# Issuing 28 stores of a two-layer spectral and MLP kernel from GpSimd in place of SyncE

## The chip, the cores and the metric

The kernel runs on one core of a Trainium2 chip. The metric is the device time of one execution in microseconds (us). The kernel before took 1453.88 us as the median of three runs, which lay between 1451.45 and 1456.33 us.

## What is computed

The reference applies two different blocks in turn, and the pair of them twice (two "layers"). `S` is 2048 tokens, `D` is 512 channels, everything is fp32.

```python
# block A: Fourier mixing, real part of a DFT over tokens of a DFT over channels
a = einsum("bsd,ed->bse", x, dft_hid_re);  b = einsum("bsd,ed->bse", x, dft_hid_im)
y = einsum("ts,bse->bte", dft_seq_re, a) - einsum("ts,bse->bte", dft_seq_im, b)
# block B: spatial shift and MLP
h  = gelu(layernorm(x) @ w1);  hs = concat(four quarters of h, shifted by +1, -1, +2, -2) @ w2
x1 = x + hs
x  = x1 + gelu(layernorm(x1) @ w3) @ w4          # w3: 512 x 1376, w4: 1376 x 512
# x = x + A(layernorm(x)); x = x + B(layernorm(x)); and both once more
```

## The kernel before

**Precision.** Every fp32 operand of a product is split into a rounded high part, written by ScalarE (ACT) as `fp32r`, and a low part, the operand less its high part, written by VectorE (DVE). One product is then three matmuls (high by high, high by low, low by high; `mm3`, L343 to L345). TensorE (PE) therefore has almost all of the work, and DVE and ACT feed it with splits, with sums and with gelu.

**Seven products in place of eight.** The large products are done on 2 x 2 blocks with seven block products in place of eight. Each needs sums of the blocks of its operands, here called forms. For the Fourier block of layer 1 the right operand is the DFT matrix of the channels (`hs`, its real and imaginary part). Its seven forms never change, so the kernel computes them once, beside other work, splits each into high and low, and keeps the results in device memory, in the tensors `hsd`. Layer 1 loads them from there (`rawr<-hsd`, from 801 us on).

**Where that is done.** The second half of a layer, the MLP with `w3` and `w4`, goes through the tokens in two pairs of chunks (`by_pairs`). In the second pair of layer 0 PE walks through the 11 blocks of `w3`, two columns at a time: for each it does seven products with `w3b` (`prod`, in the order b1, b6, b5, b2, b7, then two blocks of the product with `w4`, then b4, b3). DVE adds the seven results up out of PSUM (`rest`, L567), ACT applies gelu (L763) and splits. Between these products the code calls `one()`, which takes the next item of a list of background work, `bg`. The seven forms are on that list: `hs_forms` makes them in four quarters, and each quarter (`hs_quarter`) has one load step and five parts. In each quarter:

- `load_m` (L1208) loads the imaginary part's block into `m`, `load_r` (L1211) the real part's into `r`, 256 KB each. There is one buffer of each per quarter, and the four quarters' buffers lie at the same addresses, so a load waits until the quarter ahead has read its last values out of them.
- `sums` (L1214 to L1217, by the helper at L567) makes the sums, three of them in the buffers `hp0`, `hp1` and `hp2` (the list `fp`; the name in the trace is `hp`, its first digit the buffer and its second the quarter). These too lie at the same addresses in all quarters.
- four parts follow, which `outs` makes. Each has a step `highs_` (ACT, L1224) and a step `lows_` (DVE, L1229), and `lows_` also issues the store of the finished form to `hsd` (L1230). The parts use `hp1, hp2, hp0`, then `hp1, hp2`, then `hp0`, then `hp1`: seven forms through three buffers. A buffer is written again only when the store from it has landed, so ACT waits for stores within a quarter, and the first sum of the next quarter (into `hp1`) waits for the seventh store of the quarter ahead.

Each store moves 128 rows of 2 KB, 256 KB; there are 28 of them. The list `bg` carries the highs and lows beside steps that prepare layer 1 (`xp_stats`, `xp_norm`, `ax_sums` and so on). Of these `xp_stats` ends on GpSimd (POOL) with two small operations on a 128 x 2 tile (L362, L363), whose results ACT needs for L391.

**Queues.** Every engine works through its instructions in order. All transfers before the change are issued by SyncE (SP), in the order of the code: a transfer whose data isn't ready holds up all that stand behind it in SP. In this part SP also issues the loads of `w4` (`w4r<-w4d`, L943, 512 KB each), of `w3` (`w3b<-w3d`, L958, 1792 KB each) and the two loads of `hs`. In the code, the next quarter's `load_m` is called right behind the sixth store, and `load_r` right behind the seventh.

Of the kernel before, what the change touches and what calls it, by code (L numbers as in the profile page):

```python
# [8 lines left out]
F32 = mybir.dt.float32  # L9
# [36 lines left out]
def spectral_mlp_kernel(ctx: ExitStack, tc: tile.TileContext, x, ws, hs, w1, w2, w34, out):  # L46
    nc = tc.nc
# [110 lines left out]
    def piece(src, a=0, b=2):  # L158
        pieces.append((src, a, b))
        return len(pieces) - 1  # L160
# [25 lines left out]
    for layer in range(LAYERS):  # L186
        for c in range(NC):
# [15 lines left out]
            for k in range(NP):  # L203
# [4 lines left out]
                p = piece(ws[c, k][:, 2:4])  # L208
# [357 lines left out]
    def add(o, a, b, op=ALU.add):  # L566
        nc.vector.tensor_tensor(o, a, b, op=op)  # L567
# [290 lines left out]
    def by_pairs(layer, zs, xin, dst):  # L858
# [344 lines left out]
        def hs_quarter(m, r, fp, places):  # L1203
            b11, b12, b21, b22 = (t[:, :, v] for t in (m, r) for v in (left, right))
            raw = [tf[:, :, 1] for _, tf in fp]

            def load_m():
                nc.sync.dma_start(m, places[0][1])  # L1208

            def load_r():  # L1210
                nc.sync.dma_start(r, places[0][2])  # L1211

            def sums():
                add(raw[1], b12, b11, ALU.subtract)  # L1214
                add(raw[2], b22, b12, ALU.subtract)
                add(raw[0], b22, raw[1], ALU.subtract)
                add(b12, raw[0], b21, ALU.subtract)  # L1217

            def outs(*which):
                which = [(i, n, raw[i] if src is None else src) for i, n, src in which]  # L1220

                def highs_():
                    for i, _, src in which:
                        act(fp[i][0][:, :, 0], src)  # L1224

                def lows_():
                    for i, n, src in which:
                        t = fp[i][0]
                        nc.vector.tensor_tensor(t[:, :, 1], src, t[:, :, 0].bitcast(F32), op=ALU.subtract)  # L1229
                        nc.sync.dma_start(places[n][0].rearrange("p i (l w) -> p i l w", l=2), t.bitcast(F32))  # L1230

                return highs_, lows_

            nothing = lambda: None
            parts = [
                (nothing, sums),
                outs((1, 3, None), (2, 4, None), (0, 2, None)),
                outs((1, 0, b11), (2, 1, b12)),
                outs((0, 6, b21)),
                outs((1, 5, b22)),  # L1240
            ]
            return [(load_m, load_r), *parts]
# [15 lines left out]
        for pair in range(n_pairs):  # L1258
# [62 lines left out]
            for p in range(NF // 2):  # L1321
                prep = {} if kept else w_prep(p)
                u, v, x, y = sets[p % 2]
                w = w3b[(5 * pair + p) % 2]
# [835 lines left out]
```

## Time and profile before

| | us |
|---|---|
| median of three runs | 1453.88 |
| profiled execution | 1454.98 |
| span from its first to its last instruction | 1452.9 |
| PE busy | 1420.9 |
| DVE busy | 1204.9 |
| ACT busy | 731.8 |
| POOL busy | 76.6 |

The profiled execution gives all durations. Times inside it count from the start of the span. A row such as `647.65 0.39 SPq L1230 DMA_DIRECT2D hsd<-hp x1` gives the start, the duration in us, the engine (`SPq` is SyncE's queue of instructions), the line of the kernel, the operation, the tile written and the tile read, and how many instructions were merged. In brackets behind a row stands how long the engine was idle before it, and what ended the idle time. The issue of a transfer is short; when its data has landed is told apart, as the time from issue to landing. In the chain of waits a row with `DMA` is a transfer on its way, from issue to landing.

### The profile page before, as it was taken

Reading aid. Unit: us, or ns where it says so; the run is one execution under the profiler, and the core shown is the slowest. Engines: PE = TensorE matmul, PEld = TensorE weight load, DVE = VectorE, ACT = ScalarE, POOL = GpSimd, SP = SyncE. Lnnn points to the kernel's source line nnn. Section 1 sums busy time; section 2 is a strip of 40 time slices with the busy share of each in tenths; the row PEclk is TensorE's granted clock in tenths of the full one; section 3 lists DMA queues with packets and bytes.
Section 4 is the critical chain, followed back from the end, with each engine's and each line's share of the span. In section 5 each row is a group of like instructions: output and inputs, shape, how many; then the busy total and the mean of one; then the engine's idle time right before and its main releaser. Section 6 shows DMA issues by size and latency. Waiting matters only on the chain.

```text
span 1452.9 us, 18506 instructions
## 1 busy us (share of the span) xinstructions
PE 1420.9 (98%) x6681; PEld 1188.4 (82%) x6681; DVE 1204.9 (83%) x1725; ACT 731.8 (50%) x1020; POOL 76.6 (5%) x105
## 2 busy tenths in 40 slices
PE   9999999999999999998999989989989999999999
PEld 7888888888888888876888878878878888899887
DVE  7986998989978897667799878879879797897676
ACT  5663554445566654344555443444445666444342
POOL 2100000000002000000000000000000011000000
PEclk9999999999999999999999999999999999999999
DMA  7867657568645758877655577576687537586864
GB/s 247 274 204 234 200 173 261 173 200 296 226 133 161 268 214 282 329 251 263 232 173 190 203 256 225 187 269 222 207 294 240 173 102 275 165 250 217 320 205 163
DMA packets 145628, 325.24 MB, mean 224 GB/s; under 512 B 10624, under 2 KB 61568, under 8 KB 142848
## 3 DMA queue, kind: packets, MB, share of 16 engines
q1 hardware_dynamic: 145536, 324.05, 66.9%
q8 instruction: 53, 0.87, 0.2%
q14 instruction: 39, 0.32, 0.1%
HBM read 262.41 MB, written 61.60 MB: 223 GB/s over the span
## 4 chain that ended last, share of the span: by engine, by line
PE 83%; DVE 9%; DMA 4%; ACT 2%; issue 2%; SPq 0%; DVEq 0%; ACTq 0%
PE psd L343 8%; PE psd L345 8%; PE psd L344 8%; PE psa L343 7%; PE psa L344 7%; PE psa L345 7%; PE psb L344 6%; PE psb L343 6%; PE psb L345 6%; PE psc L344 6%; PE psc L345 6%; PE psc L343 6%; DVE ring L300 1%; DVE rest L567 1%; DMA raw<-in_ws 1%
## 5 line engine op out<-in xcount | busy, mean ns | idle before, releaser
L300 DVE TENSOR_TENSOR ring<-raw,ring 128x1024 fp32r<-128x1024 f32 x102 | 124.2, 1220 | 19.0 <-ACT ring L279 18.7
L279 ACT CAST ring<-raw 128x1024 fp32r<-128x1024 f32 x103 | 107.8, 1051 | 56.3 <-PE psd L345 25.6
L383 POOL TENSOR_TENSOR rs<-ve,mhalf 128x4 f32<-128x4 f32 x16 | 25.0, 1562 | 746.1 <-DVE nm L382 746.1
L343 PE MATMUL psd<-ring,ay 128*128 128x512 f32 x126 | 50.1, 398 | 7.8 <-DVE tmp L567 7.8
L300 DVE TENSOR_TENSOR ring<-ring1f,ring 128x512 fp32r<-128x512 f32 (+1 forms) x56 | 53.3, 952 | 2.9 <-ACT ring L282 2.9
L286 ACT CAST ring<-ring0f 128x1024 fp32r<-128x1024 f32 x28 | 29.5, 1053 | 50.5 <-DVE ring0f L285 50.2
L286 ACT CAST ring<-ring2f 128x1024 fp32r<-128x1024 f32 x28 | 29.6, 1056 | 48.8 <-DVE ring2f L285 48.8
L343 PE MATMUL psd<-rawr,hf 128*128 128x256 f32 x168 | 47.7, 284 | 5.8 <-issue 4.8
L343 PE MATMUL psc<-ring,ay 128*128 128x512 f32 x128 | 50.2, 392 | 2.0 <-ACT rr11f L608 1.7
L300 DVE TENSOR_TENSOR ring<-ring3f,ring 128x1024 fp32r<-128x1024 f32 (+1 forms) x50 | 49.3, 986 | 3.0 <-ACT ring L282 2.6
L362 POOL TENSOR_TENSOR rs<-ve,mhalf 128x2 f32<-128x2 f32 (+2 forms) x33 | 29.2, 886 | 426.6 <-DVE nb L361 407.6
L391 ACT ACTIVATE tmp<-xs,nb,rs 128x512 f32<-128x512 f32 x56 | 43.3, 810 | 15.8 <-POOL nb L363 12.6
L344 PE MATMUL psb<-ring,ay 128*128 128x512 f32 x128 | 50.3, 393 | 0.8 <-DVE ring L300 0.8
L343 PE MATMUL psb<-ring,ay 128*128 128x512 f32 x128 | 50.5, 394 | 0.0
L345 PE MATMUL psb<-ring,ay 128*128 128x512 f32 x128 | 50.1, 391 | 0.0
L345 PE MATMUL psd<-ring,ay 128*128 128x512 f32 x126 | 49.9, 396 | 0.0
L344 PE MATMUL psc<-ring,ay 128*128 128x512 f32 x128 | 49.8, 389 | 0.0
L345 PE MATMUL psc<-ring,ay 128*128 128x512 f32 x128 | 49.8, 389 | 0.0
L344 PE MATMUL psd<-ring,ay 128*128 128x512 f32 x126 | 49.8, 395 | 0.0
L344 PE MATMUL psa<-ring,ay 128*128 128x512 f32 x126 | 49.0, 389 | 0.0
L343 PE MATMUL psa<-ring,ay 128*128 128x512 f32 x126 | 49.0, 389 | 0.0
L345 PE MATMUL psa<-ring,ay 128*128 128x512 f32 x126 | 49.0, 389 | 0.0
(896 smaller groups left out, 4757.8 us busy)
## 6 DMA issues: line engine op xcount, KB each, us to landing
raw<-in_ws SPq DMA_DIRECT2D x183, 512.0 KB, 5.2
w4r<-w4d SPq DMA_DIRECT2D x44, 512.0 KB, 5.3
rawr<-hsd SPq DMA_DIRECT2D x42, 512.0 KB, 4.8
w3b<-w3d SPq DMA_DIRECT2D x10, 1792.0 KB, 9.3
raw<-in_hs SPq DMA_DIRECT2D x32, 512.0 KB, 4.0
w3d<-w3b SPq DMA_DIRECT2D x5, 1792.0 KB, 7.0
hsd<-hp SPq DMA_DIRECT2D x28, 256.0 KB, 2.4
x1d<-tmp SPq DMA_DIRECT2D x12, 512.0 KB, 7.4
```

Source lines behind the costliest of these rows:

```text
L279: nc.scalar.copy(dest[:, a:b, 0], r[0][:, a:b])
L286: nc.scalar.copy(dest[:, :, 0], lo)
L300: nc.vector.tensor_tensor(lo, src, hi.bitcast(F32), op=ALU.subtract)
L343: nc.tensor.matmul(o, lh, rh, start=first, stop=False, skip_group_check=more)
L344: nc.tensor.matmul(o, lh, rl, start=False, stop=False, skip_group_check=more)
L345: nc.tensor.matmul(o, ll, rh, start=False, stop=last, skip_group_check=more)
L362: nc.gpsimd.tensor_tensor(rs[:, :n], ve[:, :n], mhalf[:, 0, :n], op=ALU.pow)
L383: nc.gpsimd.tensor_tensor(rs, ve, mhalf[:, :, :2], op=ALU.pow)
L391: nc.scalar.activation(o, s, AF.Identity, bias=mr[2], scale=mr[1])
L567: nc.vector.tensor_tensor(o, a, b, op=op)
```

## The change

The stores at L1230 are issued by GpSimd. The operation, the data and the place in the code stay; nothing else in the kernel is edited.

```diff
                     for i, n, src in which:
                         t = fp[i][0]
                         nc.vector.tensor_tensor(t[:, :, 1], src, t[:, :, 0].bitcast(F32), op=ALU.subtract)
-                        nc.sync.dma_start(places[n][0].rearrange("p i (l w) -> p i l w", l=2), t.bitcast(F32))
+                        nc.gpsimd.dma_start(places[n][0].rearrange("p i (l w) -> p i l w", l=2), t.bitcast(F32))
```

PE, DVE and ACT keep their instructions in the same order. SP loses 28 transfers and POOL gains them. This is what stands on SP in the second quarter; `hsd_95` and the like are the seven forms, `hp_4396` is `hp1`, `hp_4398` is `hp2`, `hp_4394` is `hp0`, `hs_4400` is the next quarter's `m` and `hs_4401` its `r`.

```order
-L1230 DMA hsd_95<-hp_4396 128x512
-L1230 DMA hsd_97<-hp_4398 128x512
-L1230 DMA hsd_93<-hp_4394 128x512
-L1230 DMA hsd_89<-hp_4396 128x512
-L1230 DMA hsd_91<-hp_4398 128x512
 L943 DMA w4r_251<-w4d_114 128x1024
-L1230 DMA hsd_101<-hp_4394 128x512
 L1208 DMA hs_4400<-in_hs 128x512
 L943 DMA w4r_253<-w4d_115 128x1024
-L1230 DMA hsd_99<-hp_4396 128x512
 L1211 DMA hs_4401<-in_hs 128x512
 L958 DMA w3b_236<-w3d_86 128x3584
```

Five loads of the quarter stay on SP in their order, and no store stands between them; what `load_m` and `load_r` waited for by their place behind a store they now wait for by semaphores of DVE. On POOL the same seven stores now stand between the statistics of two steps:

```order
 L362 TENSOR_TENSOR rs<-ve,mhalf 128x2
 L363 TENSOR_TENSOR nb<-nb,rs 128x2
+L1230 DMA hsd_95<-hp_4396 128x512
+L1230 DMA hsd_97<-hp_4398 128x512
+L1230 DMA hsd_93<-hp_4394 128x512
+L1230 DMA hsd_89<-hp_4396 128x512
+L1230 DMA hsd_91<-hp_4398 128x512
+L1230 DMA hsd_101<-hp_4394 128x512
+L1230 DMA hsd_99<-hp_4396 128x512
 L362 TENSOR_TENSOR rs<-ve,mhalf 128x2
 L363 TENSOR_TENSOR nb<-nb,rs 128x2
```

The stores are queued behind the two operations of their own quarter's statistics and ahead of those of the next quarter. The other three quarters look the same.

## The prediction

> **What bounds the kernel now.** The page first: PE has almost no idle time over the whole span.
>
> ```profile
> span 1452.9 us, 18506 instructions
> PE 1420.9 (98%) x6681; PEld 1188.4 (82%) x6681; DVE 1204.9 (83%) x1725; ACT 731.8 (50%) x1020; POOL 76.6 (5%) x105
> ```
>
> So a change can gain only where PE waits. The stretches around the stores come next: busy time of each engine from the first store's quarter to the last one's, and behind it.
>
> ```profile
> 612.00:690.00 78.00, 70.35 (x299) 56.47 (x298) 56.05 (x122) 37.44 (x73) 4.01 (x8) 0.98 0.69 246
> 690.00:800.00 110.00, 109.97 (x485) 90.46 (x484) 98.57 (x141) 59.05 (x82) 6.25 (x8) 1.00 0.59 197
> ```
>
> PE (first figure after the length) idles 78.00 - 70.35 = 7.65 us in the part with the stores and not at all in the 110 us behind it. What is won or lost by 690 therefore stays. The timeline of PE shows the five waits:
>
> ```profile
> 642.23 0.50 PE L343 MATMUL psa<-b,w3b 128*128 128x512 f32 x1 [0.66 <-DVE rest L567]
> 647.25 0.50 PE L343 MATMUL psa<-bt,w3b 128*128 128x512 f32 x1 [0.63 <-DVE rest L567]
> 661.48 0.50 PE L343 MATMUL psa<-b,w3b 128*128 128x512 f32 x1 [3.05 <-DVE rest L567]
> 666.50 0.50 PE L343 MATMUL psd<-bt,w3b 128*128 128x512 f32 x1 [0.65 <-DVE rest L567]
> 680.33 0.79 PE L343 MATMUL psd<-b,w3b 128*128 128x512 f32 x1 [2.67 <-DVE rest L567]
> ```
> ```profile
> 680.00:690.00 10.00, 9.67 (x36) 7.85 (x37) 7.88 (x16) 7.18 (x14) 0.00 (x0) 0.83 0.63 209
> ```
>
> All wait for DVE's additions out of PSUM. The last wait has a second price: in the ten us from 680 on the granted clock (third figure from the end) is 0.83, so of the 9.67 us that PE is busy 0.17 x 9.67 = 1.6 us are lost.
>
> DVE is late because it waits itself. Its waits in this part, and the longest of them in its own timeline:
>
> ```profile
> DVE hp12f L567 <- DMA hsd<-hp: 3.7, 1, 3.7
> DVE hp13f L567 <- DMA hsd<-hp: 3.2, 1, 3.2
> DVE hp11f L567 <- DMA hsd<-hp: 2.4, 1, 2.4
> ```
> ```profile
> 645.84 0.75 DVE L1229 TENSOR_TENSOR hp<-hs,hp 128x256 fp32r<-128x256 f32 x2
> ...
> 653.82 0.43 DVE L567 TENSOR_TENSOR hp12f<-hs 128x256 f32<-128x256 f32 x1 [3.72 <-DMA hsd<-hp]
> ```
>
> At the turn of each quarter DVE must rewrite `hp1`, and the seventh store has not left it. At the second turn the last low is ready at 645.84 + 0.75 = 646.59 and the next quarter begins at 653.82. SP and the chain of waits show where these 7.23 us go:
>
> ```profile
> 646.29 0.32 SPq L1230 DMA_DIRECT2D hsd<-hp  x1
> 646.66 0.42 SPq L1208 DMA_DIRECT2D hs<-in_hs  x1
> 647.18 0.38 SPq L943 DMA_DIRECT2D w4r<-w4d  x1
> 647.65 0.39 SPq L1230 DMA_DIRECT2D hsd<-hp  x1
> 648.09 0.47 SPq L1211 DMA_DIRECT2D hs<-in_hs  x1
> 648.66 0.44 SPq L958 DMA_DIRECT2D w3b<-w3d  x1
> ```
> ```profile
> 629.65 4.66 DMA hsd<-hp
> ...
> 648.09 6.22 DMA hs<-in_hs
> ```
>
> The store waits 1.06 us for its turn on SP behind a store and two loads, and is then about 6 us on its way, since those transfers are ahead of it. `load_r`, issued behind it, lands at 654.31, just as late. At the first turn the store took 4.66 us.
>
> **The change, part by part.** No operation is added or removed; 28 issues move from SP to POOL. On SP they cost 0.36 us each and land in 2.0 us at the least:
>
> ```profile
> L1230 SPq DMA_DIRECT2D hsd<-hp x28: 319/357/411, 619.7 to 685.3; - x28
> DMA to landing us min/median/max: 2.0/2.4/6.0
> ```
>
> SP's 28 x 0.36 = 10 us are worth nothing by themselves; no engine waits in this part for the `w4` and `w3` loads that come earlier. What counts are `load_m` and `load_r`. `load_m` needs only forms 4 and 5, so it and the `w4` load go some 2 us earlier, and `load_r` goes as soon as the last low is read. It is no longer late.
>
> The **price of a store on POOL** stands in no row, since POOL issues nothing now. Nearest rows: the operations of the same queue.
>
> ```profile
> L362 POOL TENSOR_TENSOR rs<-ve,mhalf 128x2 f32<-128x2 f32 (+2 forms) x33 | 29.2, 886 | 426.6 <-DVE nb L361 407.6
> L383 POOL TENSOR_TENSOR rs<-ve,mhalf 128x4 f32<-128x4 f32 x16 | 25.0, 1562 | 746.1 <-DVE nm L382 746.1
> ```
>
> The bounds are 0.36 us (as on SP, landing in 2.0) and 1.56 us (landing in 2.0 + 1.56 - 0.36 = 3.2). I take 0.89 us, the row of the operation that POOL does between these very stores, and so 2.0 + 0.89 - 0.36 = 2.53 us to landing.
>
> *Within a quarter this costs.* The first store stands behind the statistics, which it did not on SP, and ACT waits for the buffers:
>
> ```profile
> 620.34 0.20 POOL L363 TENSOR_TENSOR nb<-nb,rs 128x2 f32<-128x2 f32 x1
> 639.62 0.20 POOL L363 TENSOR_TENSOR nb<-nb,rs 128x2 f32<-128x2 f32 x1
> ```
> ```profile
> 621.90 0.41 ACT L1224 CAST hp<-hs 128x256 fp32r<-128x256 f32 x1 [3.19 <-DMA hsd<-hp]
> 622.48 0.41 ACT L1224 CAST hp<-hs 128x256 fp32r<-128x256 f32 x1 [0.17 <-DMA hsd<-hp]
> ...
> 642.74 0.70 ACT L1224 CAST hp<-hs 128x256 fp32r<-128x256 f32 x2
> ...
> 645.67 0.41 ACT L1224 CAST hp<-hs 128x256 fp32r<-128x256 f32 x1 [0.50 <-DMA hsd<-hp]
> ```
>
> First quarter: stores from 620.54, 621.43; the second lands at 623.96, and the cast of 622.48 starts at 624.05, 1.55 us late. All behind it on ACT and DVE slips as much. PE doesn't wait in this quarter, so I count nothing for it here; without that slack it would be 1.55 us. Later quarters have work in front of the casts: with stores from 639.82 on the second lands at 643.24 (needed at 643.05, 0.3 late), and the fourth, ready at 643.59, at 646.1, so that the cast of 645.67 is 0.5 late. The last low is then ready at 647.1 and not 646.59. POOL's own next statistics come some 9 us after the seventh store's issue and lose nothing; stores of over 2 us each would reach them, and ACT's normalisation (L391) behind them.
>
> *At the turn it gains.* The seventh store starts on POOL at 647.6, behind the sixth. Alone it lands at 650.1. But `w3b`, 1792 KB, now leaves SP right behind `load_r`, also at 647.6, and nothing holds it back. How long it fills the queues:
>
> ```profile
> w3b<-w3d SPq DMA_DIRECT2D x10, 1792.0 KB, 9.3
> ```
> ```profile
> 652.00:658.00 6.00, 6.00 (x28) 4.99 (x27) 3.95 (x12) 1.02 (x3) 0.01 (x1) 1.00 0.91 379
> ```
>
> At 379 GB/s it takes 1.835 MB / 379 = 4.8 us. If its data start 1 us after the issue and all go first, the store lands at 648.6 + 4.8 + 1.2 = 654.6. The turn then ends between 650.2 (3.6 early) and 654.7 (0.9 late). No row says how two queues share; I take the middle, 652.5, **1.3 us early**. The first turn by the same steps: last low at 630.4, the seventh store from 630.4 lands between 632.9 and 638.0, middle 635.5, where it landed at 629.65 + 4.66 = 634.31: 1.2 late.
>
> The Trainium skill has a rule for this, "DMA: Bandwidth & Descriptors", section "Issuing engines are not separate DMA queues": transfers from all engines run on the same 16 DMA engines and interleave, and issuing from several saves only the sequencers' time. By it nothing but the 1.06 us of SP's turn is to be had at each turn, 3 us at most in all, and the store doesn't overtake for free. The 379 GB/s row, with the DMA engines 0.91 busy, leaves little room for a transfer beside `w3b`, so far in agreement.
>
> *Sum.* The third turn comes 1.2 - 1.3 - 1.3 = 1.4 us earlier than before, and PE's last wait ends with it, as its first matmul follows the turn by a fixed chain. PE's third and fourth waits shrink, but the second and fourth grow by the 0.5 of the casts; the last one is left with about 1 us. Whether the 1.6 us of the lower clock go with it is open: behind the longer wait at 661.48 the matmul took 0.50, not 0.79. I count 0.6. Together -2.0 us: 1454.98 - 2.0 = 1453.0 for the profiled execution, which lay 1.1 above the median, so **1452**.
>
> **Rivals.**
>
> *The store keeps ahead of `w3b`* (the low end). Then the turns come 1.4, 5 and 8.6 us earlier, DVE leads, and nearly all of the 7.65 + 1.6 us go; less 1.8 for what the casts still cost, 7.5: 1446. For it: the sixth store and `load_r` go first too. Against: `w3b` is issued at the same moment.
>
> *`w3b` goes first.* Turns 3.7, 4.6 and 5.5 late: 1459.
>
> *POOL is the bound*: its issues come one behind another, three at the start of each quarter, and two casts wait for them. At 1.56 us the first quarter's cast is 2.9 late and the later lows 2.1; the seventh store is issued 2 us later. With the middle share the turns come 3.6, 4.8 and 6.0 late: 1460, **slower**. Between -1.4 at 0.89 us and +6.0 at 1.56 it decides at about 1.0 us per store. For it: ACT already waits 3.19 us for a store. Against: SP's 0.36.
> The Trainium skill, "SBUF — State Buffer", section "SBUF: two separate sides", holds that GpSimd can't write its descriptors while DVE runs an operation that takes both ports. By it the price rises above 1.0 us. The quoted DVE rows here have two inputs, and no run here shows such a lock, so it has a small part of this rival.
>
> *Nothing changes*: stores land as before and `load_r` too. The span stays within 1 us: 1454.
>
> **How the numbers follow.** The forecast has 0.40 (1447 to 1455), the store ahead 0.20, `w3b` first 0.14, POOL the bound 0.22, no change 0.04. A measurement of this kernel tells about 0.3%, 4.4 us, from no change. Faster by more: 0.20 and 0.10 of the forecast, 0.30. Slower by more: 0.20 of POOL's and 0.09 of `w3b` first, 0.29. The rest, 0.41, is within. The range runs from the store ahead, 1445, to POOL's price at its upper bound, 1461.
>
> **What would show it.** Right: POOL's stores about 0.9 us apart, landing in 2.5 us within the quarter; `load_r` no longer the last; ACT's cast of the first quarter near 624; DVE's wait at the second turn near 3 us; PE's idle from 612 to 690 about 5 to 6 us. Wrong: stores over 1 us apart, casts that wait for them in every quarter, or a seventh store that lands within 3 us beside `w3b`, or only behind it.

## The result and the profile after

The changed kernel takes 1466.13 us (median of four runs, 1463.97 to 1468.90), beside 1452.86 us for the kernel before (median of four runs, 1451.45 to 1456.33). The ratio is 1.0085, with a 95% interval of 1.0066 to 1.0103: **slower by 0.85%**, 12 us, and outside the predicted range.

The page of the changed kernel and its busy time in the two stretches that the prediction read:

```profile
span 1465.1 us, 18509 instructions
PE 1428.1 (97%) x6681; PEld 1194.9 (82%) x6681; DVE 1204.9 (82%) x1725; ACT 732.1 (50%) x1020; POOL 93.6 (6%) x133
```
```profile
612.00:690.00 78.00, 63.90 (x259) 49.91 (x257) 47.44 (x106) 29.61 (x59) 16.68 (x31) 0.96 0.62 219
690.00:800.00 110.00, 108.56 (x469) 89.00 (x470) 96.79 (x146) 62.95 (x92) 9.67 (x14) 0.98 0.60 200
```

The span is 12.2 us longer, and these 188 us hold nearly all of it. PE idled 7.68 us in them before (7.65 and 0.03); now it idles 14.10 + 1.44 = 15.54, so 7.9 us more. The granted clock (third figure from the end) was 0.98 and 1.00 and is 0.96 and 0.98. Time lost to it, 1 less the clock times the length, goes from 1.6 to 3.1 + 2.2 = 5.3 us, 3.7 more; the clock has two digits, so this is good to a microsecond or so. Together 11.6.

PE's timeline shows both parts:

```profile
627.08 0.50 PE L343 MATMUL psd<-b,w3b 128*128 128x512 f32 x1 [1.39 <-DVE rest L567]
...
646.73 0.50 PE L343 MATMUL psa<-b,w3b 128*128 128x512 f32 x1 [3.61 <-DVE rest L567]
...
648.63 0.63 PE L344 MATMUL psd<-b,w3b 128*128 128x512 f32 x1
649.06 0.63 PE L345 MATMUL psd<-b,w3b 128*128 128x512 f32 x1
...
654.49 0.50 PE L343 MATMUL psa<-bt,w3b 128*128 128x512 f32 x1 [1.74 <-DVE rest L567]
...
667.68 0.50 PE L343 MATMUL psa<-b,w3b 128*128 128x512 f32 x1 [2.02 <-DVE rest L567]
...
691.26 0.50 PE L343 MATMUL psd<-b,w3b 128*128 128x512 f32 x1 [3.59 <-DVE rest L567]
```

The waits are for the same releaser as before, DVE's additions out of PSUM, but there are more of them (eight in place of five) and the longest are longer. The one of 1.39 us lies in the first quarter, where PE did not wait before. Some 2 us behind the wait of 3.61 us the matmuls start 0.43 us apart (648.63, 649.06) in place of 0.23.

DVE's timeline has the starts of the quarters:

```profile
615.16 0.42 DVE L567 TENSOR_TENSOR hp10f<-hs 128x256 f32<-128x256 f32 x1
639.25 0.43 DVE L567 TENSOR_TENSOR hp11f<-hs 128x256 f32<-128x256 f32 x1 [5.71 <-issue]
660.20 0.42 DVE L567 TENSOR_TENSOR hp12f<-hs 128x256 f32<-128x256 f32 x1 [2.85 <-issue]
683.79 0.43 DVE L567 TENSOR_TENSOR hp13f<-hs 128x256 f32<-128x256 f32 x1 [6.54 <-issue]
```

("issue" stands where the view found no releaser. The seventh store's landing, below, is 0.4, 0.1 and 0.1 us ahead of these starts.) Before, the quarters started at 616.07, 634.74, 653.82 and 672.60. The three of them took 56.5 us and now take 68.6: 12.1 more, as much as the span grew.

How a quarter divides tells where: from its first sum to the end of the last low, and from there to the next quarter, which is the seventh store's time.

| us | to the last low | then the store | sum |
|---|---|---|---|
| before | 12.8, 11.9, 12.0 | 5.9, 7.2, 6.8 | 56.5 |
| after | 14.9, 14.6, 13.5 | 9.2, 6.4, 10.0 | 68.6 |

So **about half of the loss (6.4 us) arises within the quarters, and half (5.7) at the turns**.

**At the turns.** The seventh stores of the first and the third quarter, and the `w3b` issued beside the third, each with its time from issue to landing:

```profile
L1230 POOL DMA_DIRECT2D hsd<-hp x1: 542/542/542, 630.4 to 630.4; - x1
DMA to landing us min/median/max: 8.4/8.4/8.4
```
```profile
L1230 POOL DMA_DIRECT2D hsd<-hp x1: 542/542/542, 674.1 to 674.1; - x1
DMA to landing us min/median/max: 9.6/9.6/9.6
```
```profile
L958 SPq DMA_DIRECT2D w3b<-w3d x1: 444/444/444, 674.2 to 674.2; - x1
DMA to landing us min/median/max: 9.7/9.7/9.7
```

At the third turn 256 KB land with the 1792 KB that left at the same moment. At the first turn `w3b`, issued 0.05 us behind the store, landed in 8.2 us; at the second, issued 0.29 us behind it, in 7.7, and there the store took 5.9. Before, on SP, the store left 1.0 us ahead of `w3b` (647.65 and 648.66) and landed in 6.0. `load_r` lands in 2.8 to 5.3 us and is no longer late, as predicted.

**Within a quarter.** POOL and SP from the second quarter's first store on, and ACT's casts of the seventh form in the second and third quarter:

```profile
644.47 1.73 POOL L1230 DMA_DIRECT2D hsd<-hp  x3
648.50 1.14 POOL L1230 DMA_DIRECT2D hsd<-hp  x2 [2.30 <-DVE hp L1229]
651.26 0.54 POOL L1230 DMA_DIRECT2D hsd<-hp  x1 [1.61 <-DVE hp L1229]
654.24 0.54 POOL L1230 DMA_DIRECT2D hsd<-hp  x1 [2.44 <-DVE hp L1229]
```
```profile
648.52 0.33 SPq L1208 DMA_DIRECT2D hs<-in_hs  x1
648.97 0.36 SPq L943 DMA_DIRECT2D w4r<-w4d  x1
653.86 0.33 SPq L1211 DMA_DIRECT2D hs<-in_hs  x1
654.53 0.32 SPq L958 DMA_DIRECT2D w3b<-w3d  x1
```
```profile
652.97 0.40 ACT L1224 CAST hp<-hs 128x256 fp32r<-128x256 f32 x1 [3.23 <-DMA hsd<-hp]
...
672.88 0.41 ACT L1224 CAST hp<-hs 128x256 fp32r<-128x256 f32 x1 [1.94 <-DMA hsd<-hp]
```

Before, `load_m` and the `w4` load left SP at 646.66 and 647.18, behind the sixth store. Now they leave at the moment of the fourth (648.50), whose buffer, `hp1`, ACT needs for the seventh form. The fourth store takes 4.4 us, and 3.4 in the third quarter; the cast that waited 0.50 us now waits 3.23 and 1.94. In the last quarter, where no `load_m` follows, the same store takes 2.3.

### The profile page after: what moved, and what is told of

It is laid out like the page before. It is cut to its first block, busy times and chain, and to the rows that moved or that the text cites. A ratio compares the mean times of both kernels' runs of the same rounds, so it can differ in the third digit from the quotient of the medians.

```text
span 1465.1 us, 18509 instructions
## 1 busy us (share of the span) xinstructions
PE 1428.1 (97%) x6681; PEld 1194.9 (82%) x6681; DVE 1204.9 (82%) x1725; ACT 732.1 (50%) x1020; POOL 93.6 (6%) x133
## 4 chain that ended last, share of the span: by engine, by line
PE 78%; DVE 11%; issue 4%; DMA 4%; ACT 3%; POOL 0%; SPq 0%; DVEq 0%; ACTq 0%; POOLq 0%
PE psd L343 8%; PE psd L345 8%; PE psd L344 8%; PE psa L343 6%; PE psa L344 6%; PE psa L345 6%; PE psb L344 6%; PE psb L343 6%; PE psb L345 6%; PE psc L344 6%; PE psc L345 6%; PE psc L343 6%; DVE ring L300 2%; DMA raw<-in_ws 1%; DMA hsd<-hp 1%
## 5 line engine op out<-in xcount | busy, mean ns | idle before, releaser
L279 ACT CAST ring<-raw 128x1024 fp32r<-128x1024 f32 x103 | 107.9, 1051 | 54.2 <-PE psd L345 24.9
```

What stands on the lines that cost most here:

```text
L279: nc.scalar.copy(dest[:, a:b, 0], r[0][:, a:b])
```

## Experiments

Two theories stood against each other. **Order:** a store that has no place ahead of a large load is passed by it, whichever engine issues it; the change took the stores out of SP's order, in which they held the loads back. **Software queue:** what GpSimd issues is served late by itself. Ratios are to the kernel before, run alongside (median 1452.9 us for after, 1454.8 to 1455.1 us for the numbered kernels), with 95% intervals. "Lows" and "store" are the two columns of the table above, summed over three quarters of the one profiled execution of each kernel, whose time is the last column. It can lie over 3 us from the median (1455.0 beside 1458.5 us in experiment 4), so the sums tell how that execution divides its time and not by how much the median moves.

| kernel | median us | ratio | lows | store | sum | profiled us |
|---|---|---|---|---|---|---|
| before | 1454.8 | 1 | 36.7 | 19.9 | 56.5 | 1455.0 |
| after | 1466.1 | 1.0085 (1.0066 to 1.0103) | 43.0 | 25.6 | 68.6 | 1466.9 |
| 1 seventh behind `w3b`, on SP | 1471.3 | 1.0114 (1.0085 to 1.0143) | 36.5 | 35.2 | 71.7 | 1470.6 |
| 2 seventh alone on POOL | 1455.3 | 1.0010 (1.0000 to 1.0020) | 37.8 | 19.4 | 57.2 | 1458.4 |
| 3 seventh alone on ACT | 1455.2 | 1.0004 (0.9994 to 1.0014) | 38.0 | 16.2 | 54.2 | 1455.1 |
| 4 after, seventh on SP | 1458.5 | 1.0028 (1.0013 to 1.0043) | 45.3 | 10.7 | 56.0 | 1455.0 |
| 5 after, sixth and seventh on SP | 1457.4 | 1.0019 (1.0009 to 1.0030) | 40.1 | 18.5 | 58.5 | 1458.4 |
| 6 after, `w3b` cut to a seventh | 1461.3 | 1.0033 (1.0019 to 1.0047) | 45.2 | 14.6 | 59.9 | 1463.2 |
| 7 after, `w3b` on POOL | 1460.6 | 1.0035 (1.0022 to 1.0048) | 45.9 | 13.0 | 58.9 | 1458.7 |
| 8 after, `load_m` called later | 1466.7 | 1.0081 (1.0066 to 1.0096) | 42.9 | 24.2 | 67.1 | 1466.7 |
| 9 after, second `w4` behind `load_r` | 1464.8 | 1.0064 (1.0049 to 1.0078) | 42.5 | 22.7 | 65.2 | 1463.4 |
| 10 before, second `w4` behind `load_r` | 1451.8 | 0.9973 (0.9964 to 0.9983) | 36.7 | 16.5 | 53.1 | 1454.5 |
| 11 before, both `w4` behind `load_r` | 1451.8 | 0.9985 (0.9971 to 0.9999) | 40.3 | 12.6 | 53.0 | 1451.2 |
| 12 as 11, seventh on ACT | 1452.2 | 0.9979 (0.9965 to 0.9992) | 38.1 | 14.6 | 52.7 | 1452.7 |

**1. The seventh store behind `w3b`, without GpSimd.**

```diff
+                        put = lambda n=n, t=t: nc.sync.dma_start(places[n][0]..., t.bitcast(F32))
+                        late.append(put) if n == 5 else put()
...
                 nc.sync.dma_start(w3b[i].bitcast(F32), w3d[n % (NF // 2)])
+                for put in late: put()
+                late.clear()
```

> Before, all stores on SyncE and nothing on GpSimd, but the seventh store of each of the first three quarters is issued behind w3b. Theory of order: the loss of after needs no GpSimd at all; behind the 1792 KB the store lands 8 to 11 us after its issue, each turn comes 4 to 6 us later than before, the quarters take 66 to 74 us and the time is 1464 to 1472. Rival: a small transfer is served beside a large one whatever their order, and the late landing of after comes from GpSimd's queue; then it lands in 3 to 6 us, the quarters take 55 to 60 us, the time is 1453 to 1458.

DVE's timeline of this kernel:

```profile
638.91 0.43 DVE L567 TENSOR_TENSOR hp11f<-hs 128x256 f32<-128x256 f32 x1 [7.26 <-DMA hsd<-hp]
663.00 0.42 DVE L567 TENSOR_TENSOR hp12f<-hs 128x256 f32<-128x256 f32 x1 [8.73 <-DMA hsd<-hp]
687.06 0.42 DVE L567 TENSOR_TENSOR hp13f<-hs 128x256 f32<-128x256 f32 x1 [8.71 <-DMA hsd<-hp]
```

The three stores take 8.7, 10.1 and 10.2 us, and the time rises by 1.1%. No store is on GpSimd, and the lows are as before (36.5). Landing, quarters and time are as the theory of order had them. One transfer's place behind `w3b` is enough for a loss as large as the change's. That the store waited for `w3b` in the changed kernel too is what experiments 6 and 7 show; experiment 4 agrees.

**2 and 3. The seventh store alone on another engine.**

```diff
-                        nc.sync.dma_start(places[n][0]..., t.bitcast(F32))
+                        (nc.gpsimd if n == 5 else nc.sync).dma_start(places[n][0]..., t.bitcast(F32))
```

(nc.scalar in place of nc.gpsimd for the third kernel.)

> Before, but the seventh store alone is issued by GpSimd; the other six stay on SyncE. Order: most of the loss is here, since this is the store that w3b passes: it lands 6 to 10 us after its issue, the quarters take 62 to 68 us, the time is 1459 to 1466. Software queue: one store of seven costs a small part, the quarters take under 60 us and the time is 1453 to 1457.

> Before, but the seventh store is issued by ScalarE; the other six stay on SyncE. Order: what counts is that it left the queue of w3b, not that GpSimd issues it; the store lands 5 to 10 us after its issue at the turns and the time is within 4 us of the kernel in which GpSimd issues the seventh alone, 1458 to 1466. Software queue: from an engine with a queue like SyncE's it lands in 2 to 3.5 us, the quarters are no longer than before and the time is 1449 to 1455.

"Order" missed both times. "Software queue" has its time from POOL, but not its landing of 2 to 3.5 us from ACT: the store takes 5.8 to 6.2 us from POOL and 4.2 to 5.2 from ACT, and neither kernel is slower by as much as 0.3%. What I had overlooked stands in SP's timeline of the second kernel; POOL issues the store at 647.25:

```profile
646.63 0.32 SPq L1230 DMA_DIRECT2D hsd<-hp  x1
647.00 0.42 SPq L1208 DMA_DIRECT2D hs<-in_hs  x1
647.52 0.38 SPq L943 DMA_DIRECT2D w4r<-w4d  x1
647.99 0.42 SPq L1211 DMA_DIRECT2D hs<-in_hs  x1
648.51 0.43 SPq L958 DMA_DIRECT2D w3b<-w3d  x1
```

The sixth store still holds `load_m` and `w4` back, and their issues with that of `load_r` keep `w3b` 1.26 us behind the seventh store. In after `load_m` and `w4` had left 4 us or more before the store, and `w3b` was 0.05, 0.29 and 0.00 us behind. So it isn't the queue of the seventh store by itself that costs; the stores together had spaced the loads on SP.

**4 and 5. The last one or two stores back on SP, the others on GpSimd.**

```diff
-                        nc.gpsimd.dma_start(places[n][0]..., t.bitcast(F32))
+                        (nc.sync if n == 5 else nc.gpsimd).dma_start(places[n][0]..., t.bitcast(F32))
```

(`n in (5, 6)` for the fifth kernel; `n == 6` is the sixth store.)

> After, but the seventh store of each quarter (form 5) goes back to SyncE; the other six stay on GpSimd. Two theories. Order: a store that does not stand ahead of w3b on its own queue is passed by it; then the seventh store, ahead of load_r and w3b again, lands within 6 us of its issue and the three quarters take 50 to 60 us (56.5 before, 68.6 after), the time is 1449 to 1458. What can stay of the loss is the fourth store, which load_m and w4 pass as they leave SP together with it. Software queue: what GpSimd issues is late by itself; then six of seven stores stay late, the quarters take over 62 us and the time is over 1460.

> After, but the sixth and seventh store of each quarter are on SyncE; the first five stay on GpSimd. Theory of order: what the change took away is that these two stores hold back, on SyncE, the loads of the code behind them (load_m and w4 behind the sixth, load_r and w3b behind the seventh). With both back, the fourth store lands in 2.3 to 3 us, the casts behind it no longer wait over 1 us, the quarters take 55 to 57.5 us and the time is 1453 to 1456. Software queue: the first five stores of GpSimd still come late, the casts wait for the fourth as when the seventh alone is back (2.8 and 2.0 us) and the time stays at 1457 to 1460.

With the seventh store back, it lands in 2.7 to 3.6 us, the turns cost 10.7 us in place of 25.6, and two thirds of the loss is gone. The time of 1458.5 us lies half a microsecond above what "order" had, and below "software queue". The lows stay late, and the fourth store, at 644.0, shows why, here beside `load_m` and `w4`:

```profile
L1230 POOL DMA_DIRECT2D hsd<-hp x1: 539/539/539, 644.0 to 644.0; - x1
DMA to landing us min/median/max: 4.2/4.2/4.2
```

With the sixth back as well, `load_m` leaves at 648.12, behind it, and the same store of GpSimd takes:

```profile
L1230 POOL DMA_DIRECT2D hsd<-hp x1: 539/539/539, 645.0 to 645.0; - x1
DMA to landing us min/median/max: 2.3/2.3/2.3
```

In the later quarters the lows come 0.6 and 0.7 us later than before, and 2.1 in the first. Five of seven stores on GpSimd cost 0.19% (2.8 us). The sixth's leaving SP raises this to 0.28% (the intervals overlap), the seventh's to 0.85%. The time, 1457.4 us, lies where "software queue" had it, above the 1453 to 1456 of "order"; but its reason, a fourth store that stays late, falls with the 2.3 us, and the casts behind it wait 1.1 us at most. What is left is mostly the first quarter's slip, for which PE waits as in after:

```profile
626.99 0.50 PE L343 MATMUL psd<-b,w3b 128*128 128x512 f32 x1 [1.40 <-DVE rest L567]
```

Before, PE had no wait there, and from 612 to 690 it idles 9.25 us here in place of 7.65.

**6 and 7. Take `w3b` away, or put it behind the store.**

```diff
-                nc.sync.dma_start(w3b[i].bitcast(F32), w3d[n % (NF // 2)])
+                nc.sync.dma_start(w3b[i][:, :, 0:1].bitcast(F32), w3d[n % (NF // 2)][:, :, 0:1])
```
```diff
+                on = nc.gpsimd if layer == 0 and n > NF // 2 + 1 else nc.sync
-                nc.sync.dma_start(w3b[i].bitcast(F32), w3d[n % (NF // 2)])
+                on.dma_start(w3b[i].bitcast(F32), w3d[n % (NF // 2)])
```

(The first edit, too, holds only for layer 0 and n > NF // 2 + 1. That kernel leaves out six of the seven blocks of these loads and multiplies with old data in their place.)

> After, all stores on GpSimd, but the three w3b loads of these quarters move one block of seven, 256 KB in place of 1792 (the other six blocks are left out and old data are used). Order: nothing big is left to pass the seventh store, it lands 2.5 to 4 us after its issue, the quarters take 48 to 58 us and the time is 1445 to 1455; the fourth store's collision with load_m and w4 can stay. Software queue: the seventh store still takes over 5 us, and the time is over 1460.

> After, but the three w3b loads of these quarters are issued by GpSimd too, behind the seventh store in its queue. Theory of order: the store can't be passed any more and lands in 2.3 to 4 us beside the full 1792 KB; the quarters take 57 to 61 us and the time is 1456 to 1461, about that of the kernel with the small w3b. What is left of the loss is the fourth store's. Software queue, or w3b's large packets winning whatever the order: the seventh store still takes over 5 us, the quarters over 64 us, the time is over 1462.

The seventh store takes 3.9 to 4.8 us with the small `w3b` and 3.3 to 4.1 with the full one behind it on POOL's queue; the turns cost 14.6 and 13.0 us. Beside the full `w3b` of SP it took 8.4, 5.9 and 9.6 in after. So `w3b`'s data are most of what the store waited for. The time of the small `w3b` was expected at 1445 to 1455 and is 1461.3, which alone would fit "software queue" (over 1460); the landing doesn't. Both stay some 5 us above before, since the lows are as late as in experiment 4 (I had set the fourth store's part too low there). In the second kernel POOL issues `w3b` up to 2.2 us behind the store, so this doesn't tell the order in a queue from the distance in time:

```profile
649.77 0.55 POOL L1231 DMA_DIRECT2D hsd<-hp  x1 [1.26 <-DVE hp L1230]
651.98 0.54 POOL L959 DMA_DIRECT2D w3b<-w3d  x1 [1.66 <-issue]
```

**8 and 9. Other orders of the loads, with the stores on GpSimd.**

```diff
-                        if n < 3 and i > 2:
-                            more_.append(work[6 * n + 6][i - 3])
+                        if n < 3 and i > 3:
+                            more_ += work[6 * n + 6]
```

> After, all stores on GpSimd, but load_m stands behind the seventh low, together with load_r. Theory of order: the fourth store has only the w4 load beside it and lands in 2.3 to 3.6 us, the cast behind it waits under 1.5 us; w3b leaves one issue, 0.45 us, later, so the seventh store still lands 5 to 8 us after its issue. The quarters take 61 to 65 us, the time is 1458 to 1463. Software queue: nothing changes for the stores, the time is within 2 us of after, 1464 to 1468.

The edit didn't do what I wrote. `load_m` left at 648.86, not with `load_r` at 653.57: nothing on SP makes it wait for a store any more, only its own data do. What moved is the `w4` load, to 641.07. So this run shows the fourth store beside `load_m` alone: 3.8 us, with the cast behind it waiting 2.59. Most of the collision is `load_m`'s. The time fell where "software queue" had it, but since the edit left `load_m` beside the fourth store, this doesn't decide between the two.

The ninth kernel is after with the edit of experiment 10.

> After, all stores on GpSimd, and the second w4 load of a quarter behind load_r, ahead of w3b. Theory: a few tenths of a us decide who is first. In after w3b left 0.05, 0.29 and 0.00 us behind the seventh store, which took 8.4, 5.9 and 9.6 us; here w4 leaves at that moment and w3b one issue, 0.45 us, later: the store is passed by 512 KB and not by 1792 and lands in 4 to 6 us at the second and third turn, where w4 is moved; the fourth store has only load_m and one w4 load beside it. Quarters 62 to 66 us, time 1458 to 1463. Rival: the store from GpSimd's queue loses to w3b even so; it lands after 8 us or more at the third turn and the time is over 1464.

The quarters came out (65.2), the time did not, and the landings fit neither. `w3b` left 0.76 us behind the store at the second turn, which took 5.1 us, but 0.52 us behind at the third, where it took 7.2. In after and in the eighth kernel nothing leaves SP between the store and `w3b`: the four stores that `w3b` followed within 0.05 us landed in 8.1 to 9.6 us, the two that it followed by 0.29 and 0.37 us in 5.9 and 5.6. Those two are both at the second turn, so another cause there isn't excluded, and how large a lead keeps a store ahead stays open.

**10 to 12. The loads' order on SP, with the stores left there.**

```diff
                     w4_part(acc1, f, h, lambda: at_point(4 + i))
-                    w4_load()
+                    if not (next_too and i):
+                        w4_load()
                     one()
+                    if next_too and i:
+                        w4_load()
```

(Experiment 11 moves both `w4` loads behind `one()` of the second; 12 adds the edit of experiment 3.)

> Before, all stores on SyncE, but the second w4 load of each quarter is issued behind the seventh store and load_r (and ahead of w3b). Theory of the turn: the turn is set by the landing of the seventh store and load_r, and 512 KB ahead of them cost 1.5 to 2.5 us; the quarters take 49 to 53 us, PE idles under 5 us in place of 7.65 and the time is 1446 to 1451. Rival: PE's waits do not follow the turns alone (with the seventh store on ScalarE the quarters were 2.4 us shorter and the time the same); then the time is 1453 to 1456.

> Before, all stores on SyncE, but both w4 loads of a quarter are issued behind the seventh store and load_r, ahead of w3b. Theory of the turn: one w4 load out of the way shortened the quarters from 56.5 to 53.1 us and PE's idle from 7.65 to 4.8 us; the second gives less, since the casts and lows of a quarter take their time anyway: quarters 49 to 52 us, PE idle 2 to 4 us, time 1448 to 1452. Rival: w4 or w3b now comes late and PE waits for it; then the time is over 1454.

> As the kernel before it (both w4 loads behind load_r), and the seventh store is issued by ScalarE, so that load_m and load_r do not wait on SyncE for it. By the order of the queue load_r leaves some 0.4 us earlier, and w3b, behind two w4 loads, is over 1 us away from the store and can't pass it: the store lands in 2.5 to 4.5 us, quarters 47 to 51 us, time 1447 to 1452. Rival: w4 and w3b pass the store here too; it lands after 6 us or more and the time is over 1454.

SP's timeline of the tenth kernel in the second quarter:

```profile
645.13 0.32 SPq L1230 DMA_DIRECT2D hsd<-hp  x1
645.50 0.42 SPq L1208 DMA_DIRECT2D hs<-in_hs  x1
646.02 0.38 SPq L1230 DMA_DIRECT2D hsd<-hp  x1
646.45 0.44 SPq L1211 DMA_DIRECT2D hs<-in_hs  x1
646.99 0.42 SPq L943 DMA_DIRECT2D w4r<-w4d  x1
647.50 0.44 SPq L958 DMA_DIRECT2D w3b<-w3d  x1
```

With 512 KB moved from ahead of the seventh store and `load_r` to behind them, the turns cost 3.4 us less and PE idles 4.8 us from 612 to 690 in place of 7.65. The kernel takes **1451.8 us, 0.27% less than before** (0.17 to 0.36); the theory's ranges for the quarters' sum (49 to 53) and the time (1446 to 1451) were just missed. That the shorter turns make the lower median is argued: the profiled execution is the slowest of eleven, 0.5 us below that of before, at a mean granted clock of 0.994 beside 0.996, a difference worth some 3 us of 1453 by my estimate (0.002 x 1453). The second `w4` load brings nothing more: `w3b`, now behind 512 KB at the first turn and 1 MB at the others, lands at 640.3, 658.9 and 677.4, and beside it the first three stores of the next quarter take 3.8 to 5.6 us in place of 2.0 to 2.4. So what the turns gained (12.6 us in place of 16.5) came back in the lows (40.3 in place of 36.7). That ACT issues the seventh store changes nothing further (0.9979). The sums expected of these two, 49 to 52 and 47 to 51 us, were missed, and so was PE's idle time expected of the eleventh, 2 to 4 us: it is 7.0. The eleventh's time came out (1448 to 1452); the twelfth's (1447 to 1452) was missed by 0.2 us.

## Why the prediction was wrong

**POOL's price: right.** The 28 issues and their landing:

```profile
L1230 POOL DMA_DIRECT2D hsd<-hp x28: 542/542/747, 620.2 to 696.7; - x28
DMA to landing us min/median/max: 2.3/2.7/9.6
```

A store holds POOL 0.54 to 0.75 us (taken: 0.89), far from the 1.56 of the upper bound and below the 1.0 from which that rival decided. Alone it lands in 2.3 to 2.7 us (taken: 2.53). *POOL is the bound* falls.

**The first quarter's casts: right in place and about in size.** They start at 622.77 and 623.65, in a quarter that began 0.9 us earlier; its last low slips by 2.1 us, where I had 1.55. **"PE doesn't wait in this quarter, so I count nothing" was wrong:** the slack was smaller than the slip, and PE waits 1.39 us at 627.08, near the 1.55 that the prediction gave as the price without slack.

**Later quarters' casts, 0.5 us late: a step that failed.** Right without the loads, wrong in after. They slipped by 2.7 and 1.5 us. With the sixth and seventh store back on SP it was 0.6 and 0.7. I had seen that `load_m` and `w4` leave 2 us earlier, and had written that nothing waits for them; I didn't ask beside which store they would then travel. They travel with the fourth, the one that ACT waits for.

**The seventh store: the other step that failed.** "No row says how two queues share; I take the middle, 652.5, 1.3 us early" put its landing 4.9 us behind its issue, between 2.5 alone and 7.0 behind `w3b`. It took 8.4, 5.9 and 9.6: at two turns of three it was beyond the far bound. The turns came 4.5, 6.4 and 11.2 us later than before, where the sum had 1.2 late, 0.1 early and 1.4 early. At those two it landed within 0.2 us of `w3b` itself, as late as the rival *`w3b` goes first* had it; at the second, where `w3b` left 0.29 us behind it and not at the same moment, it landed 2.1 us ahead of `w3b`. Whether all of `w3b`'s data went first or the two shared in proportion to their size, the landings don't tell. The 1 us ahead of `w3b`'s data and the 1.2 us behind them, in the far bound, came from no row, and no run splits a landing into such parts. That rival's 1459 was too low for two reasons: the store landed up to 2.6 us behind its bound, and it had no part for the collision at the fourth store.

The row that I had weighed against a free passing was the busy one, 379 GB/s at a DMA share of 0.91. The Trainium skill, "DMA: Bandwidth & Descriptors", section "Issuing engines are not separate DMA queues", says of such transfers that they interleave; with the last two landings of after, 0.1 us apart at 256 and 1792 KB, that was no protection for the smaller one.

**The clock: wrong in sign.** I counted 0.6 us won; 3.7 were lost, since PE's waits grew instead of shrinking. DVE's wait at the second turn, 2.85 us for the 3 expected, came near by luck: the low ahead of it and the store were both later than I had them.

**The turn decides, not SP's issues: right.** That 10 us of SP's issue time were worth nothing by themselves agrees with the result, and experiment 10, whose turns are 3.4 us shorter in all, is 0.27% faster without taking anything off SP.

## What to carry to other kernels

A transfer's place in a queue does two things: it costs the ones behind it time, and it keeps them behind. Before moving transfers to another engine, list what stood behind each, when that will now leave, and what it will then travel beside; give the far bound, not the middle, to a small transfer that leaves at the same moment as a large one. If a transfer lands late, it may be cheaper to reorder the loads around it on its own queue.

## What the runs showed of the hardware

- In after a 256 KB store issued within 0.3 us of a 1792 KB load on another engine's queue landed 5.9 to 9.6 us later, and 2.3 us later with no load beside it. On one queue, 0.4 to 0.5 us behind that load (experiment 1), it landed in 8.7 to 10.2.
- The same store lands 0.3 us later from GpSimd in after (2.3 us at the least) than from SyncE before (2.0), and holds GpSimd 0.54 us in place of 0.36 for SyncE.
- From 1 to 2 us behind some of PE's longer waits the matmuls go 0.43 us apart in place of 0.23, for 2 to 3 us. What sets it off stays open: in after it follows the waits of 3.61, 2.02 and 3.59 us and none of the five below 2; in the kernel before it follows the one of 2.67 us at 680.33 and not the one of 3.05 us at 661.48.
